# Turning q and k on VectorE instead of TensorE, with 32x32 score tiles and a re-planned instruction order

## The chip, the cores and the metric

The kernel runs on one core of a Trainium2 chip. The core has a matrix engine (TensorE, PE in the profile, with PEld for its weight loads), a vector engine (VectorE, DVE), an activation engine (ScalarE, ACT), a general engine (GpSimd, POOL) and a queue engine (SyncE, SP) that issues transfers. The metric is the time on the device in microseconds.

## The reference

Nystrom attention on q, k, v of shape [8 batches, 8 heads, 576 tokens, 64], then a mixture of experts over the 4608 tokens of width 512.

```
q_lm, k_lm = means over 18 consecutive tokens (32 landmarks)
A = softmax(q k_lm^T / 8);  Bm = softmax(q_lm k_lm^T / 8);  C = softmax(q_lm k^T / 8)
Z = iterated inverse of Bm (6 steps);  x = A Z C v, heads side by side
e = argmax(x w_gate);  out = p_e * sigmoid(x w_output_gate)_e * relu(x w1[e]) w2[e]
```

There are 8 experts with w1 [512, 1024] and w2 [1024, 512]. All tensors are float32 in memory.

## The kernel before

The work goes by batch, and inside a batch by two halves of four heads. The function batch (L367 to L762) does not issue anything: it registers operations with a planner, P.op, with an assumed duration for each engine that may do it, the buffers it takes, and a priority. Plan.run (L124 to L219) is a list scheduler that runs while the kernel is built: it takes the operation that can begin first, near ties by priority, chooses the engine that ends it earliest (shy adds a handicap to an engine), and the resulting order is written out as the fixed instruction order of each engine. Attention of batch b has priority b, its feed-forward b + 3.5.

For each half:
- k, q and v come by one transfer each on SP's queue (L378), 96 partitions, six tokens of each head in a partition (1536 B runs).
- q and k are turned on PE: 24 transposes of 96x96 (L390) into the two-bank buffers S, then copied out by ACT or DVE (L345, L351) into Tq and Tk, with two tokens' 64 channels on 128 partitions.
- Sums over 18 tokens: nine by DVE (L414, L417) or POOL (L420 to L424), then the two halves of the partitions are swapped and added (sw, L435) to give the landmarks lm.
- Scores of C (L446) and of A (L491): each 8 products of 64 rows x 32 columns with 288 moving columns; a float32 product is two matmul instructions.
- C: maximum (L452), scaling (L453), exponential (L455), six transposes on PE (L463), copy ECT, product with v (L475), scaled by the reciprocal (L480, L481).
- A: 32x32 block turn on DVE (L495), maximum (L498), subtraction on POOL (L503), exponential (L505), sum and reciprocal (L509, L510), multiplication on POOL (L512), block turn back (L516) to AT.

For each batch: scores of Bm (L527) and its normalisation (L533 to L560), seven inverse steps on PE and DVE (L573, L580 to L585), the gate product (L606), logits (L618), routing on DVE (L637 to L686), and x transposed in bf16 (L699). POOL's queue then asks for the main expert's weights, cast to bf16 (w1 in three transfers, L312 and L315; w2 in one, L720); from batch 2 on they are skipped where the expert is already there. Feed-forward: up (L734) in 16 groups of four matmuls with relu on ACT (L343), down (L749) in five row blocks of eight, scaled (L756, L758) and stored by SP (L761). Tokens of other experts go through a branch at the end (L782 on).

PSUM's eight banks are split into S (two buffers of two banks), M (two, attention) and F (two, feed-forward).

Of the kernel before, what the change touches and what calls it, by code (L numbers as in the profile page):

```python
# [37 lines left out]
class Val:  # L38


    def __init__(self, tag):
        self.tag = tag
        self.slot = None
        self.users = set()
# [9 lines left out]
class Tag:  # L54
    def __init__(self, name, tiles, ordered=True):
        self.name = name
        self.tiles = tiles
        self.held = [None] * len(tiles)
        self.free_at = [0.0] * len(tiles)
        self.ordered = ordered  # L60
        self.made = []
        self.given = 0


class Op:
    __slots__ = ("engs", "fn", "deps", "new", "vals", "prio", "lag", "end", "eng", "nd", "succ", "load", "seq",
                 "mode", "bias", "shy")


class Plan:  # L70
# [3 lines left out]
    LAT = 180.0  # L74
    PE_LAG = 50.0
    SWITCH = 95.0
    WINDOW = 3410.0
    IDLE = 0.5

# [5 lines left out]
    def op(self, engs, fn, r=(), w=(), hold=(), prio=0.0, lag=0.0, load=0.0, mode=None, after=(), bias=0.0, shy=()):  # L85
        o = Op()
        o.engs, o.fn, o.prio, o.lag, o.load = engs, fn, prio, lag, load
        o.end = None
        o.mode = mode
        o.bias = bias  # L90
# [33 lines left out]
    def run(self):  # L124
# [16 lines left out]
        filled = {}  # L141
        while ready:
            cands = []
            for o in ready:
# [3 lines left out]
                for v in o.new:  # L148
                    tg = v.tag
                    if tg.ordered and tg.made[tg.given] is not v:  # L150
                        ok = False
# [71 lines left out]
def kernel(  # L223
# [28 lines left out]
    SHY = 800.0  # L252
    SHYF = 300.0
# [28 lines left out]
    t_n = {x: tag(f"n{x}", 3, [PT, HH, 6 * D]) for x in "qkv"}  # L282
    t_T = {x: tag(f"T{x}", 2, [128, 3 * HH * PT]) for x in "qk"}
    t_s3 = tag("s3", 1, [128, HH * PT])
    t_s9 = tag("s9", 2, [128, 2, 128])
    t_lm = tag("lm", 3, [128, 2, 128])
    t_sw = tag("sw", 1, [128, 2, 128])
# [5 lines left out]
    t_X = tag("X", 3, [128, 2, m + D])  # L293
    t_sm = tag("sm", 6, [128, 64])
# [15 lines left out]
    def ask_w1(dst, e, **new):  # L310
        w = moe_w1[bass.ds(e, 1)]
        nc.gpsimd.dma_start(out=dst[:, :2], in_=w.rearrange("e (c p) f -> p (e c) f", p=128)[:, :2], **new)  # L312
        src = w.rearrange("e (c a p) f -> a p (e c) f", a=2, p=D)
        for a in range(2):
            nc.gpsimd.dma_start(out=dst[a * D:(a + 1) * D, 2:], in_=src[1 - a, :, 2:], **new)  # L315

    with tc.manual_schedule():
# [7 lines left out]
        nc.gpsimd.iota(ri, pattern=[[S, B], [128, NT]], base=0, channel_multiplier=1)  # L325
        nc.vector.tensor_copy(rows, ri)
        nc.vector.tensor_scalar(out=e8, in0=e0, scalar1=8.0, scalar2=None, op0=ADD)
        for hf in range(2):
            nc.sync.dma_start(out=wgs[hf * D:(hf + 1) * D, :, :E],
                              in_=moe_w_gate[hf * HH * D:(hf + 1) * HH * D].rearrange("(h d) e -> d h e", d=D))  # L330
            nc.sync.dma_start(out=wgs[hf * D:(hf + 1) * D, :, E:],
                              in_=moe_w_output_gate[hf * HH * D:(hf + 1) * HH * D].rearrange("(h d) e -> d h e", d=D))
        nc.vector.tensor_scalar(out=wgs[:, :, E:], in0=wgs[:, :, E:], scalar1=-1.0, scalar2=None, op0=MUL)
# [19 lines left out]

        def turned(T, x):
            if x == "k":
                return T.t.rearrange("p (j n) -> p j n", j=3)
            return T.t.rearrange("p (n j) -> p j n", j=3)

# [3 lines left out]
        def dve(n=0):  # L362
            return {"DVE": 100 + max(40, 1.05 * n)}

        xTs, coms = {}, {}

        def batch(b):  # L367
            pr = float(b)
# [3 lines left out]
            vns = []  # L372
            for hf in range(2):
                pr = b + 0.1 * hf
                ns = {}
                for x, src in (("k", k), ("q", q), ("v", v)):
                    n = ns[x] = Val(t_n[x])
                    P.op({"SP": 60}, lambda e, n=n, src=src, hf=hf: nc.sync.dma_start(  # L378
                        out=n.t, in_=src[b, hf * HH:(hf + 1) * HH].rearrange("h (p t) d -> p h (t d)", t=6)),
                        w=[n[0]], prio=pr, lag=2000, load=2300)  # L380
                vns.append(ns["v"])
                Ts = {"q": Val(t_T["q"]), "k": Val(t_T["k"])}
                order = [("k", 0), ("k", 1), ("k", 2), ("q", 0), ("q", 1), ("q", 2)]
                for a in range(3):
                    tp = Val(p_S)
                    two = order[2 * a:2 * a + 2]
                    for i, (x, j) in enumerate(two):
                        def turn(e, x=x, j=j, i=i, tp=tp, n=ns[x]):
                            for h in range(HH):
                                nc.tensor.transpose(tp.t[:, i, h * PT:(h + 1) * PT],  # L390
                                                    in_=n.t[:, h, j * 128:(j + 1) * 128], identity=I128[:PT, :PT])
                        P.op({"PE": 332}, turn, r=[ns[x][0]], w=[tp[i]], hold=[Ts[y] for y, _ in two], mode=(128, 128), prio=pr + .01)
                    if two[0][0] == two[1][0]:
                        x, j = two[0]
                        T = Ts[x]
                        P.op(evac(768), copy_to(lambda T=T, j=j, x=x: turned(T, x)[:, j:j + 2],
                                                lambda tp=tp: tp.t[:, :, :HH * PT]),
                             r=[tp[0], tp[1]], w=[T[j], T[j + 1]], prio=pr + .01)
                    else:
                        for i, (x, j) in enumerate(two):  # L400
                            T = Ts[x]
                            P.op(evac(384), copy_to(lambda T=T, j=j, x=x: turned(T, x)[:, j],
                                                    lambda tp=tp, i=i: tp.t[:, i, :HH * PT]),
                                 r=[tp[i]], w=[T[j]], prio=pr + .01)
                s9 = Val(t_s9)
                for i, x in enumerate("qk"):
                    T = Ts[x]
                    s3 = Val(t_s3)

                    def sums(e, T=T, s9=s9, s3=s3, i=i, x=x):  # L410
                        f = turned(T, x)
                        if e == "DVE":
                            if x == "k":
                                nc.vector.tensor_reduce(  # L414
                                    s9.t[:, i], f.rearrange("p j (r w) -> p r j w", w=3), axis=XY, op=ADD)
                            else:
                                nc.vector.tensor_reduce(  # L417
                                    s9.t[:, i], T.t.rearrange("p (r w) -> p r w", w=9), axis=X, op=ADD)
                            return
                        nc.gpsimd.tensor_tensor(s3.t, f[:, 0], f[:, 1], op=ADD)  # L420
                        nc.gpsimd.tensor_tensor(s3.t, s3.t, f[:, 2], op=ADD)
                        c = s3.t.rearrange("p (n w) -> p n w", w=3)
                        nc.gpsimd.tensor_tensor(s9.t[:, i], c[:, :, 0], c[:, :, 1], op=ADD)
                        nc.gpsimd.tensor_tensor(s9.t[:, i], s9.t[:, i], c[:, :, 2], op=ADD)  # L424
                    P.op({"POOL": 2900, "DVE": 1350}, sums, r=[T[0], T[1], T[2]], w=[s9[i], s3[0]], prio=pr + .02, shy={"DVE": SHY})
                lm = Val(t_lm)
                lms.append(lm)
                sw = Val(t_sw)
                for c in range(2):
                    P.op({"POOL": 480, "DVE": 260, "ACT": 390},  # L430
                         copy_to(lambda c=c, sw=sw: sw.t[c * D:(c + 1) * D], lambda c=c, s9=s9: s9.t[(1 - c) * D:(2 - c) * D]),
                         r=[s9[0], s9[1]], w=[sw[c]], prio=pr + .02, shy={"DVE": SHYF})

                def folded(e, lm=lm, s9=s9, sw=sw):
                    (nc.gpsimd if e == "POOL" else nc.vector).tensor_tensor(lm.t, s9.t, sw.t, op=ADD)  # L435
                P.op({"POOL": 730, "DVE": 370}, folded, r=[s9[0], s9[1], sw[0], sw[1]], w=[lm[0]], prio=pr + .02, shy={"DVE": SHYF})

                pC = Val(p_S)
                EC = Val(t_EC)
                st = Val(t_sm)  # L440
                sms.append(st)

                def c_scores(e, pC=pC, lm=lm, T=Ts["k"]):
                    for h in range(HH):
                        for t2 in range(2):
                            nc.tensor.matmul(pC.t[h * m:(h + 1) * m, t2, :U2],  # L446
# [398 lines left out]
```

## Time and profile before

| what | value |
|---|---|
| median of three runs | 335.58 us (334.67 to 338.91) |
| profiled execution: time, span | 333.46 us, 331.8 us |
| PE busy, 4270 matmul instructions | 287.8 us |
| PEld busy | 182.8 us |
| DVE busy | 192.0 us |
| ACT busy | 174.7 us |
| POOL busy | 85.2 us |
| moved by DMA | 48.95 MB, 147 GB/s on average |

Busy time is the union of the instructions of an engine. In a group's row the columns are: line, engine, operation, output<-input, shapes and count; then busy time and mean ns of one; then the idle time just before, with what ended it. In a timeline row they are: start, duration, engine, line, operation. Matmul ends are modelled and overlap, so distances between starts tell more.

### The profile page before, as it was taken

What the parts mean: (1) busy time and instruction counts of PE and PEld (TensorE: products, weight loads), DVE (VectorE), ACT (ScalarE), POOL (GpSimd) and SP (SyncE); (2) the same over time, 40 slices, a digit from 0 to 9 for tenths busy, and PEclk for the clock granted to TensorE, in tenths of its full rate; (3) what the DMA queues carried; (4) which work ended last, traced back from release to release, by engine and by line L of the source; (5) the groups of instructions that cost most, each with busy time, mean ns of one, the idle gap of its engine ahead of it and who ended that gap; (6) DMA issues with size and microseconds to landing.
All of it is one profiled execution on the core that took longest, in us unless ns stands there. A gap on an engine that the chain in (4) does not pass through costs nothing. (4 is left out here: it accounts for less than half of the span.)

```text
span 331.8 us, 10174 instructions
## 1 busy us (share of the span) xinstructions
PE 287.8 (87%) x4270; PEld 182.8 (55%) x4281; DVE 192.0 (58%) x526; ACT 174.7 (53%) x370; POOL 85.2 (26%) x126
## 2 busy tenths in 40 slices
PE   0576868799979989899978998999999998999994
PEld 0545655566656665657644575666565555454551
DVE  1258928977987388729866669784968626000000
ACT  1344526537845457537654566465764345454542
POOL 1034642237153024214331402330221311010000
PEclk9999779769999999999999999999999999999999
DMA  4999999289999978076730455665000946949103
GB/s 96 247 247 245 250 213 233 49 187 227 229 182 232 261 225 193 9 212 178 167 85 2 134 154 123 139 104 167 2 18 2 219 84 99 177 113 200 51 33 112
DMA packets 33584, 48.95 MB, mean 147 GB/s; under 512 B 2816, under 2 KB 26368, under 8 KB 33536
## 3 DMA queue, kind: packets, MB, share of 16 engines
q1 hardware_dynamic: 25536, 37.79, 44.4%
q0 software_dynamic: 8000, 10.49, 19.7%
q8 instruction: 34, 0.56, 0.7%
q14 instruction: 14, 0.11, 0.1%
HBM read 61.90 MB, written 9.44 MB: 215 GB/s over the span
## 5 line engine op out<-in xcount | busy, mean ns | idle before, releaser
L734 PE MATMUL F<-xT_all,w 128*128 128x288 bf16 x512 | 76.1, 286 | 2.1 <-ACT y L756 1.1
L749 PE MATMUL F<-w,hT 128*128 128x512 bf16 (+1 forms) x310 | 73.2, 380 | 1.0 <-ACT y L756 0.3
L734 PEld LDWEIGHTS <-w 128*128 128x128 bf16 x512 | 47.4, 98 | 24.1 <-issue 11.7
L343 ACT ACTIVATE hT<-F 128x288 bf16<-128x288 f32 x128 | 50.0, 411 | 16.8 <-PE F L734 14.9
L749 PEld LDWEIGHTS <-hT 128*128 128x128 bf16 (+1 forms) x320 | 30.7, 100 | 35.0 <-issue 2.8
L756 ACT ACTIVATE y<-F,co 128x512 f32<-128x512 f32 (+1 forms) x38 | 26.1, 686 | 42.4 <-PE F L749 36.6
L390 PE MATMUL S<-I,nk 96*128 96x96 f32 x192 | 25.2, 275 | 14.2 <-DMA nk<-in_k_dram 11.2
L573 PE MATMUL M<-X 32*32 32x96 f32 x768 | 26.5, 251 | 5.3 <-issue 3.2
L503 POOL TENSOR_TENSOR At<-At,sm 128x576 f32<-128x576 f32 x16 | 18.5, 1156 | 49.1 <-DVE sm L498 27.5
L390 PEld LDWEIGHTS S<-I,nk 96*128 96x128 f32 x192 | 21.1, 160 | 17.1 <-issue 9.0
L345 ACT COPY Tq<-S 128x768 f32<-128x768 f32 (+1 forms) x23 | 22.9, 1004 | 11.1 <-PE S L390 11.1
L390 PE MATMUL S<-I,nq 96*128 96x96 f32 x192 | 24.6, 270 | 2.1 <-DVE Tk L351 1.8
L345 ACT COPY Tk<-S 128x384 f32<-128x384 f32 (+1 forms) x25 | 15.6, 633 | 20.0 <-PE S L390 19.5
L512 POOL TENSOR_TENSOR At<-At,sm 128x576 f32<-128x576 f32 x16 | 18.5, 1159 | 28.2 <-DVE sm L510 10.3
L583 DVE SCALAR_TENSOR_TENSOR X<-X,M 128x192 f32<-128x192 f32 x40 | 13.7, 344 | 19.6 <-PE M L573 19.4
L573 PEld LDWEIGHTS M<-X 32*32 32x32 f32 x768 | 15.7, 105 | 16.7 <-issue 7.8
L417 DVE TENSOR_REDUCE s<-Tq 128x128 f32<-128x1152 f32 x14 | 18.9, 1350 | 8.8 <-ACT Tq L345 8.7
L390 PEld LDWEIGHTS S<-I,nq 96*128 96x128 f32 x192 | 20.4, 156 | 5.7 <-DVE Tk L351 2.4
L345 ACT CAST xT_all<-S 128x576 bf16<-128x576 f32 x28 | 16.7, 641 | 11.3 <-PE S L699 11.2
L455 ACT ACTIVATE EC<-S,sm 128x576 f32<-128x576 f32 x16 | 11.8, 740 | 18.3 <-DVE sm L453 16.7
L435 POOL TENSOR_TENSOR lm<-s,sw 128x256 f32<-128x256 f32 x12 | 8.7, 725 | 41.1 <-ACT sw L345 34.4
L345 ACT COPY ECT<-S 96x768 f32<-96x768 f32 x14 | 11.1, 796 | 14.9 <-PE S L463 14.8
(118 smaller groups left out, 395.0 us busy)
## 6 DMA issues: line engine op xcount, KB each, us to landing
nk<-in_k_dram SPq DMA_DIRECT2D x16, 576.0 KB, 8.8
nq<-in_q_dram SPq DMA_DIRECT2D x16, 576.0 KB, 8.4
nv<-in_v_dram SPq DMA_DIRECT2D x16, 576.0 KB, 8.0
w<-in_moe_w_dram POOLq DMA_DIRECT2D x8, 1024.0 KB
out_dram<-y SPq DMA_DIRECT2D x32, 256.0 KB, 2.7
w<-in_moe_w_dram POOLq DMA_DIRECT2D x8, 512.0 KB
w<-in_moe_w_dram POOLq DMA_DIRECT2D x16, 256.0 KB
out_dram<-y SPq DMA_DIRECT2D x8, 128.0 KB, 2.4
```

What stands on the lines that cost most here:

```text
L343: nc.scalar.activation(out=dst(), in_=src(), func=RELU)
L345: nc.scalar.copy(dst(), src())
L390: nc.tensor.transpose(tp.t[:, i, h * PT:(h + 1) * PT], in_=n.t[:, h, j * 128:(j + 1) * 128], identity=I128[:PT, :PT])
L417: nc.vector.tensor_reduce(s9.t[:, i], T.t.rearrange("p (r w) -> p r w", w=9), axis=X, op=ADD)
L455: P.op({"ACT": 900}, lambda e, pC=pC, EC=EC, st=st: nc.scalar.activation(out=EC.t, in_=pC.t[:, :, :U2], func=EXP, scale=s_a, bias=st.t[:, ...
L503: P.op({"POOL": 1160}, lambda e, At=At, st=st: nc.gpsimd.tensor_tensor(At.t, At.t, b_l(st.t[:, 8:8 + g]), op=SUB), r=[st["ax"]], w=[At[0]] ...
L512: P.op({"POOL": 1160}, lambda e, At=At, st=st: nc.gpsimd.tensor_tensor(At.t, At.t, b_l(st.t[:, 32:32 + g]), op=MUL), r=[st["as"]], w=[At[0 ...
L573: nc.tensor.matmul(pN.t[r_, hf * W:(hf + 1) * W], lhsT=cur.t[r_, hf, :m], rhs=cur.t[r_, hf, :])
L583: nc.vector.scalar_tensor_tensor(out=nxt.t, in0=cur.t, scalar=2.0, in1=p3, op0=MUL, op1=SUB)
L734: nc.tensor.matmul(ph.t[:, :NH], lhsT=w1.t[:, dc, fc * 128:(fc + 1) * 128], rhs=xT.t[:, dc, n * NH:(n + 1) * NH], start=(dc == 0), stop=(d ...
L749: nc.tensor.matmul(py.t[:tk, :], lhsT=hTs[fc].t[:, i * 128:i * 128 + tk], rhs=w2.t[:, fc, :], start=(fc == 0), stop=(fc == FCH - 1))
L756: nc.scalar.activation(out=y.t[:tk], in_=py.t[:tk, :], func=COPY, scale=com.t[:tk, i:i + 1])
```

## The change

- q and k come with 18 tokens of one head and landmark in a partition (128 partitions, 4608 B runs). DVE turns them in 32x32 blocks straight into Tq and Tk, whose partitions are (head, 32 channels), with the two channel halves side by side. PE no longer turns them and no engine copies them.
- The sums of 18 tokens are taken from the loaded layout by five adds on POOL or DVE, and then turned once by DVE into lm.
- Both scores become one operation of 32 float32 products of 32 rows x 32 columns, in two accumulated channel halves. It takes both S buffers. C's rows are rotated by two heads.
- v comes in three transfers, with tokens in an order that suits ECT. Tokens then stand in (18, 32) order down to the output, whose store picks rows 18 apart.
- w1 and w2 are asked for in halves; up and down wait for the half that they need.
- The gate weights are loaded after the second half's inputs, no longer first.
- M and F become one pool of four banks, attention and feed-forward capped at two each; from batch 5 on the feed-forward may take four.
- The planner has other latencies and priorities, counts PE's instruction records, and lets a fetch of 256 take no less than 3.8 us. The inverse of batch 0 is done in two halves. C's scaling moves to ACT, some small copies may go to ACT or POOL.

```diff
-    LAT = 180.0
-    PE_LAG = 50.0
+    LAT = 90.0
+    PE_LAG = 150.0
+    CHUNK = 256
+    FETCH = 3800.0
...
+                if recs // self.CHUNK != (recs + o.recs) // self.CHUNK:
+                    part = (self.CHUNK - recs % self.CHUNK) / o.recs
+                    at = max(st + part * (en - st), chunk_at + self.FETCH)
+                    en = at + (1.0 - part) * (en - st)
+                    chunk_at = at
+                recs += o.recs
...
+    PR = [0.0, 1.0, 2.0, 3.0, 4.0, 5.0, 6.0, 7.0]
+    FR = [3.5, 4.5, 5.5, 5.25, 7.5, 8.5, 9.5, 10.5]
+    PESUM = 0
+    SPLIT = (0,)
+    CAPA = 2
+    CAPF = 2
+    LASTF = 5
...
-    p_M = tag("M", 2, [128, 512], ps=True, ordered=False)
-    p_F = tag("F", 2, [128, 512], ps=True, ordered=False)
+    p_M = tag("M", 4, [128, 512], ps=True, ordered=False)
...
+                        if x == "v":
+                            for w in range(3):
+                                nc.sync.dma_start(out=n.t[w * m:(w + 1) * m],
+                                                  in_=s_.rearrange("h (r w t) d -> w r h (t d)", w=3, t=6)[w])
+                        else:
+                            nc.sync.dma_start(out=n.t, in_=s_.rearrange("h (r t) d -> (h r) t d", t=g))
...
-                            for h in range(HH):
-                                nc.tensor.transpose(tp.t[:, i, h * PT:(h + 1) * PT],
-                                                    in_=n.t[:, h, j * 128:(j + 1) * 128], identity=I128[:PT, :PT])
+                for x in "kq":
+                    P.op({"DVE": 1370}, lambda e, T=Ts[x], n=ns[x], x=x: nc.vector.transpose(
+                        out=T.t.rearrange("p j (t r) -> p t j r", r=m) if x == "q" else
+                        T.t.rearrange("p j (t w r) -> p w t j r", t=6, w=3),
+                        in_=n.t.rearrange("p t (j c) -> p t j c", j=2) if x == "q" else
+                        n.t.rearrange("p (w t) (j c) -> p w t j c", j=2, w=3)),
+                        r=[ns[x][0]], w=[Ts[x][0]], prio=pr + .01)
...
+                    def sums(e, n=ns[x], s9=s9, s3=s3, i=i):
+                        eng = nc.gpsimd if e == "POOL" else nc.vector
+                        eng.tensor_tensor(s3.t, n.t[:, :9], n.t[:, 9:], op=ADD)
+                        eng.tensor_tensor(s3.t[:, :4], s3.t[:, :4], s3.t[:, 4:8], op=ADD)
+                        eng.tensor_tensor(s3.t[:, :2], s3.t[:, :2], s3.t[:, 2:4], op=ADD)
+                        eng.tensor_tensor(s3.t[:, 0], s3.t[:, 0], s3.t[:, 1], op=ADD)
+                        eng.tensor_tensor(s9.t[:, i], s3.t[:, 0], s3.t[:, 8], op=ADD)
+                    P.op({"POOL": 3200, "DVE": 1750}, sums, r=[ns[x][0]], w=[s9[i], s3[0]], prio=pr + .005, shy={"DVE": SHY})
...
+                def scores(e, pC=pC, pA=pA, lm=lm, Ts=Ts):
+                    for n in range(2):
+                        for j in range(2):
+                            for h in range(HH):
+                                r_ = slice(h * m, (h + 1) * m)
+                                o = (h + 2) % HH
+                                nc.tensor.matmul(pC.t[o * m:(o + 1) * m, n, :U2], lhsT=lm.t[r_, 0, j, :],
+                                                 rhs=Ts["k"].t[r_, j, n * U2:(n + 1) * U2], start=(j == 0), stop=(j == 1))
+                                nc.tensor.matmul(pA.t[r_, n, :U2], lhsT=lm.t[r_, 1, j, :],
+                                                 rhs=Ts["q"].t[r_, j, n * U2:(n + 1) * U2], start=(j == 0), stop=(j == 1))
...
-            P.op({"POOL": 1200}, ask1, r=[em[0]], w=[w1[0]], prio=pr + .06, lag=2000, load=8100)
+            for part in range(2):
+                P.op({"POOL": 1500}, lambda e, part=part: ask1(e, part), r=[em[0]], w=[w1[part]], hold=[w2], prio=pr + .06,
+                     lag=2000, load=WLOAD / 2)
...
-                    out=out[b * S + i * 128:b * S + i * 128 + tk, :], in_=y.t[:tk]), r=[y[0]], prio=fr, lag=2000, load=900)
+                    out=out[b * S:(b + 1) * S].rearrange("(r t) d -> t r d", t=g)[HH * i:HH * i + tk // m], in_=y.t[:tk]), r=[y[0]], prio=fr, lag=2000, load=900)
```

More of the change, by code (lines that the diff above doesn't have):

```diff
@@ L89, in op @@
         o.mode = mode
+        o.recs = recs
         o.bias = bias
@@ L150, in run @@
                     if tg.ordered and tg.made[tg.given] is not v:
+                        ok = False
+                        break
+                    if sum(x is not None and x.kind == v.kind for x in tg.held) >= v.cap:
                         ok = False
@@ L352, in copy_to, with bring_gates @@
             return emit
[L354 to L357, printed above, removed]
         def evac(n):
             return {"ACT": 140 + 0.95 * n, "DVE": 90 + 1.1 * n}
-        def dve(n=0):
-            return {"DVE": 100 + max(40, 1.05 * n)}
         xTs, coms = {}, {}
+        gates = Val(None)
+        def bring_gates(e):
+            for hf in range(2):
+                for i, w in enumerate((moe_w_gate, moe_w_output_gate)):
+                    nc.sync.dma_start(out=wgs[hf * D:(hf + 1) * D, :, i * E:(i + 1) * E],
+                                      in_=w[hf * HH * D:(hf + 1) * HH * D].rearrange("(h d) e -> d h e", d=D))
         def batch(b):
-            pr = float(b)
+            pr = PR[b]
             lms, ATs, sms, ZVp = [], [], [], []
@@ new lines, in batch @@
+                    P.op({"SP": 550 if x != "v" else 1500}, bring, w=[n[0]], prio=pr if x != "v" else pr + .15, lag=2000, load=LOAD)
+                if b == 0 and hf == 1:
+                    P.op({"SP": 2500}, bring_gates, w=[gates[0]], prio=pr, lag=2500)
+                    P.op({"POOL": 400}, lambda e: nc.gpsimd.tensor_scalar(
+                        out=wgs[:, :, E:], in0=wgs[:, :, E:], scalar1=-1.0, scalar2=None, op0=MUL),
+                        w=[gates[0]], prio=pr + .5)
+                Ts = {"q": Val(t_T["q"]), "k": Val(t_T["k"])}
@@ L426, in batch @@
                 lm = Val(t_lm)
                 lms.append(lm)
[L428 to L435, printed above, removed]
@@ L436, in batch @@
[L436 to L438 removed]
+                P.op({"DVE": 270}, lambda e, lm=lm, s9=s9: nc.vector.transpose(
+                    out=lm.t.rearrange("p x j r -> p (x j r)"),
+                    in_=s9.t[:, :128] if b < PESUM else s9.t.rearrange("p x d -> p (x d)")),
+                    r=[s9[0], s9[1]], w=[lm[0]], prio=pr + .02)
+                pC, pA = Val(p_S), Val(p_S)
@@ L439, in batch @@
                 EC = Val(t_EC)
+                At = Val(t_At)
                 st = Val(t_sm)
                 sms.append(st)
[L443 to L446, printed above, removed]
-                                             lhsT=lm.t[t2 * D:(t2 + 1) * D, 0, h * m:(h + 1) * m],
-                                             rhs=turned(T, "k")[t2 * D:(t2 + 1) * D, :, h * PT:(h + 1) * PT])
@@ new lines, in c_rec @@
+                def c_rec(e, st=st):
+                    for a in range(2):
+                        nc.vector.reciprocal(st.t[a * D:(a + 1) * D, 3:4], st.t[(1 - a) * D:(2 - a) * D, 2:3])
+                P.op({"DVE": 280}, c_rec, r=[st[1]], w=[st[2]], prio=pr + .035)
+                def pv_out(e, pV=pV, st=st, hf=hf):
+                    if e == "ACT":
+                        nc.scalar.activation(out=XW.t[:, hf, m:], in_=pV.t[:, :D], func=COPY, scale=st.t[:, 3:4])
+                    else:
+                        nc.vector.tensor_scalar(out=XW.t[:, hf, m:], in0=pV.t[:, :D], scalar1=st.t[:, 3:4],
+                                                scalar2=None, op0=MUL)
@@ L725, in batch @@
+            for part in range(2):
+                P.op({"POOL": 1500}, lambda e, part=part: ask1(e, part), r=[em[0]], w=[w1[part]], hold=[w2], prio=pr + .06,
+                     lag=2000, load=WLOAD / 2)
+            for part in range(2):
+                P.op({"POOL": 500}, lambda e, part=part: ask_w2(w2.t, reg["e"], part, **reg["new"]),
+                     r=[w1[0], w1[1]], w=[w2[part]], prio=pr + .06, lag=2000, load=WLOAD / 2)
+            fr = FR[b]
             hTs = []
@@ L780 @@
     gi = pool.tile([128, NT], I32, name="gi")
-    xg = pool.tile([128, DCH, S], BF16, name="xg")
+    xg = t_hT.tiles[FCH:FCH + DCH]
     with tc.If(strays > 0):
         with tc.For_i(0, B) as bi:
-            nc.vector.tensor_copy(xg, xT_all[:, bass.ds(bi, 1)].rearrange("p a c s -> p (a c) s"))
+            for dc in range(DCH):
+                nc.vector.tensor_copy(xg[dc], xT_all[:, bass.ds(bi, 1), dc].rearrange("p a s -> p (a s)"))
             for i, src in enumerate((eid_all, co_all, rows)):
@@ L790 @@
                 with tc.If(flag > 0):
-                    ask_w1(w1, ei_)
-                    nc.gpsimd.dma_start(out=w2, in_=moe_w2[bass.ds(ei_, 1)].rearrange("e (c p) d -> p (e c) d", p=128))
+                    for part in range(2):
+                        ask_w1(w1, ei_, part)
+                        ask_w2(w2, ei_, part)
                     nc.vector.tensor_copy(gen[:, 3, :1], e0[:, bass.ds(ei_, 1)])
```

293 lines of the change are left out of this document (130 added, 163 removed).

## Prediction, on record before the run

> **What bounds the kernel now.** I read the page's slices first, then its costliest groups, then the timeline of single engines.
>
> ```profile
> PE   0576868799979989899978998999999998999994
> DVE  1258928977987388729866669784968626000000
> PEclk9999779769999999999999999999999999999999
> DMA  4999999289999978076730455665000946949103
> ```
>
> A slice is 8.3 us. TensorE (PE) is nearly full from slice 10 to the end; the first 80 us are the weak part. VectorE (DVE) is done at 281 us, 46 us before the last matmul: what is left then is a backlog of feed-forward work on PE. So PE's work is the bound after the first 80 us, and a chain of short steps before. The table by stretches says: PE busy 55.26 of the first 80 us, 187.08 of the next 200, 45.47 of the last 52.
>
> ```profile
> L734 PE MATMUL F<-xT_all,w 128*128 128x288 bf16 x512 | 76.1, 286 | 2.1 <-ACT y L756 1.1
> L390 PE MATMUL S<-I,nk 96*128 96x96 f32 x192 | 25.2, 275 | 14.2 <-DMA nk<-in_k_dram 11.2
> L390 PE MATMUL S<-I,nq 96*128 96x96 f32 x192 | 24.6, 270 | 2.1 <-DVE Tk L351 1.8
> L417 DVE TENSOR_REDUCE s<-Tq 128x128 f32<-128x1152 f32 x14 | 18.9, 1350 | 8.8 <-ACT Tq L345 8.7
> ```
>
> The turning of q and k (L390) is a sixth of PE's busy time, and its first matmul waits 9.1 us for k. Ends of matmuls overlap, so I price PE by distances between starts, at full clock, from the timeline:
>
> ```profile
> 229.01 1.16 PE L390 MATMUL S<-I,nq 96*128 96x96 f32 x12
> 230.01 0.66 PE L734 MATMUL F<-xT_all,w 128*128 128x288 bf16 x4
> ...
> 237.45 0.53 PE L573 MATMUL M<-X 32*32 32x96 f32 x16
> 237.91 0.71 PE L446 MATMUL S<-Tk,lm 64*32 64x288 f32 x16
> 238.42 0.69 PE L491 MATMUL S<-Tq,lm 64*32 64x288 f32 x16
> 239.04 0.53 PE L573 MATMUL M<-X 32*32 32x96 f32 x16
> ...
> 272.36 0.74 PE L699 MATMUL S<-AT,X 32*64 32x288 f32 x16
> 273.03 1.15 PE L734 MATMUL F<-xT_all,w 128*128 128x288 bf16 x8
> ```
>
> Twelve turns take 1.00 us (four alone 0.33 to 0.43), the k scores 0.51, the q scores 0.62, one inverse step 0.46, half of the x product 0.67.
>
> **PE, per half batch (16 of them).** Removed: 24 turns, about 2.1 us, and both scores, about 1.15. Added: scores as 64 matmul instructions of 288 columns, 32 rows each, on 8 tiles of the array, against 16 and 16 on 8 tiles before: each tile now streams 8 instead of 2 and 2. From L446 (16 instructions on 8 tiles, 0.51) four times gives 2.04; from L699, which also uses 32-row tiles, 4 x 0.67 = 2.68. I take 2.2: L446 matches the output width of 32 columns, and L573 (32x32 tiles) shows little over its stream. Net -2.1 - 1.15 + 2.2 = -1.05, so -17 us in all (bounds -19 and -9). The small B scores double from 16 to 32 instructions: 8 x 0.15 = +1. PE falls by about 16 us.
>
> On the scores a rule stands against the change. L573 writes one bank from four row tiles at once, in different partitions; its 16 instructions of 96 columns stand 0.46 us apart, where one after the other, at L446's 0.51 / 2 = 0.255 us for 288 columns, they would need 16 x 0.085 = 1.36. So in this trace such tiles do run together. The Trainium skill, TensorEngine Tiling (Array Packing), section Gotcha 1: PSUM Pressure, says that different row tiles can't access one bank at the same time; the new scores write each bank from four row tiles, so by it they would run one by one in two banks, 64 x 0.255 / 2 = 8.2 us, not 2.2. L573 disagrees; it is a rival below.
>
> **DVE.** Removed: block sums 18.9 + 14.7 (L417, L414), copies of Tq, Tk on DVE 4.7 + 2.4 + 3.8 + 1.7, swap copies 3.1, fold 1.7, the scaling L453 2.5: 53.5 us. Added: 32 block turns of 1152 columns. The turn L516 takes 0.770 for 576 columns and L621 0.335 for 160, 1.05 ns a column, so 1.37 each, 43.9 us; the turned strides are new, so the price lies between 0.77 (half the columns) and twice 1.37. The landmark turn, 128 columns, 0.30 x 16 = 4.8. A second reciprocal, 2.2; split inverse of batch 0, about 1. Sums that the plan gives to DVE: by L435 (256 columns 0.43) and L638 (40 columns 0.20) five adds cost 0.76 + 0.43 + 0.29 + 0.23 + 0.23 = 1.9 each; I guess 8 of 32, 15 us (none to all: 0 to 61). DVE becomes 192.0 - 53.5 + 67 = 206 us, 25.7 a batch.
>
> **ACT and POOL.** ACT loses the copies of Tq, Tk and sw, 46 us of 174.7, and gets small operations at about 0.27 (L641) some 32 times, 9 us. POOL loses 32 us (fold, swap, its seven old sums) and gets about 24 sums: 1.16 + 0.73 + 0.49 + 0.4 + 0.35 = 3.1 by L503, L435, L424 and below, 74 us; twice as many weight transfers add up to 15 us of issue. POOL goes from 85 to about 142. Both have room, so their own cost is nothing beside PE; what would cost is a landmark that comes late from POOL, or the port: L663 takes 0.231 as a rule and 1.100 once, L638 0.200 and 0.770, each while a POOL add ran. Such stretches add up to 6.3 us now; with 1.7 times POOL's time, 10 to 11, +4 on DVE.
>
> The Trainium skill, SBUF, section Who interferes with whom, says that DVE instructions with two SBUF inputs lose whole instructions of time to GpSimd ones that read SBUF. The stretched rows agree, and by it DVE's new adds could each lose up to one POOL add, 1.16 us: 40 adds, at most 46 us more on DVE, against the 4 taken.
>
> **Front of the work.** Now k is issued at 3.69, behind four gate loads, and lands at 9.10. It becomes SP's first transfer, at 0.9, so 6.3; q 2.4 us later (576 KB at 245 GB/s), 8.7. Sum of k on POOL 6.3 to 9.4; turn of q on DVE 8.7 to 10.1; sum of q to 12.3; landmarks 12.6; scores 12.8 to 17 at the half clock that the first turns show (12 in 2.15). Before, they ended at 24.1, and the second half's at 31.6. The next half's k and q stand ahead of v now and land at 11.1 and 13.5; DVE's turns and POOL's sums set its scores at 18 to 22: 9.5 us earlier. The chain from there to the first feed-forward (31.6 to 79.5 now: softmax, inverse 39.3 to 53.9, routing, weights asked at 67.2) stays. Weights in halves let the up product start on half of w1, 1 MB less at 227 GB/s, 4.5 us (0 if SP's other loads fill the gap, 6 if both gain). First feed-forward: 79.5 - 9.5 - 4.5 = 65 us. v in three transfers costs SP 2 x 0.31 to 0.6 us more each, hidden by loads that run two halves ahead; gates are needed at 56 us now and load after the second half, hidden. The output goes in the same 2 KB rows to other places: 0 as long as y's four buffers cover 2.4 to 2.7 us; else 0.3 a row block.
>
> **Instruction fetch.** q8 shows 34 packets, 0.56 MB: 256 PE instructions each. The 3.15 us wait of L573 at 41.1 for "issue" is PE waiting with its data ready. PE's records go from 8551 to 9063 (-768 turns, +1024 scores, +256 B scores): two fetches more. I take 0: a stall less, two fetches more, between -3 and +6.
>
> **The sum**, on the profiled execution (span 331.8, time 333.46; the median shown is 335.58). After 79.5 PE had 5.5 batches of attention at 15.9 us (2 x (2.1 + 1.15 + 0.68 + 0.8) + 6.4) and 8 feed-forwards of 17.7 (64 x 0.135 + 40 x 0.227): 229. It took 248, factor 1.08. After the change 65 us in, with 2.07 batches done (59 us at 25.7 each, DVE nine tenths busy), there remain 5.93 x 13.9 + 142 = 224.5, by 1.08 242.5; the end after the last matmul is 4.5: 312. From batch 5 on the feed-forward may use four banks: alone, four up matmuls stand 0.576 apart (48 in 6.89), mixed 0.49; 16 such in two to three batches give 3 back. Span 309, time 311.
>
> **Rivals.**
> (1) DVE becomes the bound, and the kernel slower. Attention needs 206 us of it; after its last operation there remain weights (12.3 less 4.5), 17.7 of feed-forward and 2, about 27. If it is busy a share s, the end is 6 + 206 / s + 27. It decides at 0.69 (332); at 0.65 it is 350. Its share from 6 to 281 us now is 191 / 275 = 0.69, and my forecast needs 0.75. For it: this share, both new scores that need both S banks at once, and POOL's locks. Against: DVE reaches 0.94 and 0.95 in 30 to 40 and 80 to 90 us, and between 80 and 280 us, at 0.71, it was PE, 94% busy, that held the attention back, with 46 us of feed-forward left over at the end.
> (2) Freed PE time stays idle: the front is no earlier, scores cost 2.68, two fetches stall: 333 - 9 + 1 + 4 = 329, about no change. For it: PE waits in the first 80 us on ACT, DVE and DMA by turns. Against: the full slices behind.
> (3) It goes better: the inverse of batch 0 in halves and a plan with fetches save 8 us more of the chain, and half of the 13 us idle between 80 and 280: about 297.
> (4) Row tiles exclude each other in a bank: 16 x (8.2 - 2.2) = 96 more, over 400. L573 speaks against it.
>
> **How the numbers follow.** Forecast 0.62 (300 to 322 by the bounds of scores, DVE sums and front); (1) 0.16, of which 0.06 comes out level; (2) 0.07, of which 0.02 is faster; (3) 0.13; (4) 0.02. Faster by over 2% (below 328.9; 2% is about what a measurement can tell): 0.62 + 0.13 + 0.02 = 0.77; same 0.06 + 0.05 = 0.11; slower 0.10 + 0.02 = 0.12. The range 296 to 328 takes in (3) and the forecast's bounds.
>
> **What would show it.** Right: no L390 turns; a score group of 1024 matmuls about 2.2 us apart per half; DVE turns of 1.37; first feed-forward near 65 us; PE busy near 270; DVE near 206. Wrong: DVE turns near 2.7 us, scores near 2.7 or 8, PE waiting for DVE between 80 and 250 us, or DVE still busy 30 us before the end.

## The result, and the profile after

The changed kernel takes 339.47 us (median of 20 runs, 335.08 to 343.01) beside 335.1 us for the kernel before (20 runs, 331.49 to 340.39): ratio 1.012, 95% interval 1.008 to 1.017. The forecast was 311 us, range 296 to 328. Ratios and their intervals, here and below, are of the fast runs of each kernel alone, while medians are of all its runs, so the two differ a little. The profiled execution shown here took 341.74 us, with a span of 340.1 us and a mean granted TensorE clock of 0.913 (0.973 before).

First the slices of the changed kernel's page, 8.5 us each; they answer to the first lines shown of before.

```profile
PE   0466755896998799599899997399999975996950
DVE  4698978797897896689816936459441430500000
PEclk9956969699999799899999999789999995999795
DMA  7999747559958977476212315817021159196221
```

TensorE (PE) has holes near 140, 215 and 280 us, where it was nearly full before, and its last slice is empty. From 136 us on, each slice with a granted clock under 9 is one of these holes, comes right behind one, or is the last; in the first experiment below, a clock of 0.948, still lower than before, goes with 314 us, which speaks against the clock as a cause of its own. Now the costliest groups of the same page.

```profile
L759 PE MATMUL M<-xT_all,w 128*128 128x288 bf16 x512 | 75.2, 298 | 19.3 <-DMA w<-in_moe_w_dram 11.9
...
L459 PE MATMUL S<-Tk,lm 32*32 32x288 f32 x512 | 43.6, 467 | 11.4 <-DVE lm L442 11.4
...
L415 DVE STREAM_TRANSPOSE Tk<-nk 128x1152 f32<-128x1152 f32 x16 | 21.7, 1358 | 0.1
L415 DVE STREAM_TRANSPOSE Tq<-nq 128x1152 f32<-128x1152 f32 x16 | 21.5, 1346 | 0.0
```

The parts that the change was priced by are as priced: a turn on DVE takes 1.35 us, and PE is busy for 265.4 us (287.8 before), DVE for 199.5 (192.0), ACT for 146.3 (174.7), POOL for 137.7 (85.2). What is new is in the first row: the up products (L759) stand idle for 19.3 us, most of it for weights; before (L734) it was 2.1 us, half of it for y. The waits of PE in the changed kernel (total, times, longest) put it in order:

```profile
PE M L759 <- DMA w<-in_moe_w_dram: 11.9, 4, 4.4
...
PE M L759 <- DVE X L602: 4.3, 2, 3.4
PE M L759 <- ACT y L781: 2.9, 1, 2.9
```

Why would ACT be late with y? The timeline of ACT at the end of the changed kernel says it:

```profile
313.27 0.68 ACT L781 ACTIVATE y<-M,co 64x512 f32<-64x512 f32 x1 [5.12 <-DMA out_dram<-y]
...
325.77 0.69 ACT L781 ACTIVATE y<-M,co 128x512 f32<-128x512 f32 x1 [0.18 <-PE M L774]
328.74 0.68 ACT L781 ACTIVATE y<-M,co 64x512 f32<-64x512 f32 x1 [2.29 <-PEq L807]
```

At 313 us ACT waits 5.12 us for a store (out_dram<-y) to free one of y's four buffers, and after the last scaling, which ends at 329.4, the span goes on for 10.7 us. Before, the same row is this, and 3.9 us remain to 331.8:

```profile
327.27 0.68 ACT L756 ACTIVATE y<-F,co 64x512 f32<-64x512 f32 x1 [1.16 <-PEq L782]
```

So the theory after the look at the traces was S: the store is slow. Its rivals were W (weights are asked for too late by the new plan) and D (DVE is the new bound, rival 1 of the prediction).

### The profile page after: what moved, and what is told of

Same layout as the page of the kernel before. It is cut to its first block, busy times and chain, and to the rows that moved or that the text cites. A ratio compares the mean times of both kernels' runs of the same rounds, so it can differ in the third digit from the quotient of the medians.

```text
span 340.1 us, 10916 instructions
## 1 busy us (share of the span) xinstructions
PE 265.4 (78%) x4525; PEld 169.9 (50%) x4537; DVE 199.5 (59%) x542; ACT 146.3 (43%) x356; POOL 137.7 (40%) x225
## 5 line engine op out<-in xcount | busy, mean ns | idle before, releaser
L759 PE MATMUL M<-xT_all,w 128*128 128x288 bf16 x512 | 75.2, 298 | 19.3 <-DMA w<-in_moe_w_dram 11.9
L774 PE MATMUL M<-w,hT 128*128 128x512 bf16 (+1 forms) x309 | 73.6, 381 | 0.6
L759 PEld LDWEIGHTS <-w 128*128 128x128 bf16 x512 | 50.3, 102 | 38.5 <-issue 12.6
L365 ACT ACTIVATE hT<-M 128x288 bf16<-128x288 f32 x128 | 50.4, 410 | 31.6 <-PE M L759 27.4
L459 PE MATMUL S<-Tk,lm 32*32 32x288 f32 x512 | 43.6, 467 | 11.4 <-DVE lm L442 11.4
L461 PE MATMUL S<-Tq,lm 32*32 32x288 f32 x512 | 41.1, 465 | 0.0
L781 ACT ACTIVATE y<-M,co 128x512 f32<-128x512 f32 (+1 forms) x38 | 25.8, 685 | 34.1 <-PE M L774 24.7
L459 PEld LDWEIGHTS S<-Tk,lm 32*32 32x32 f32 x512 | 25.2, 119 | 18.3 <-DVE lm L442 11.1
L434 POOL TENSOR_TENSOR s<-nk 128x576 f32<-128x576 f32 x13 | 18.3, 1407 | 14.9 <-DMA nk<-in_k_dram 8.0
L415 DVE STREAM_TRANSPOSE Tk<-nk 128x1152 f32<-128x1152 f32 x16 | 21.7, 1358 | 0.1
L415 DVE STREAM_TRANSPOSE Tq<-nq 128x1152 f32<-128x1152 f32 x16 | 21.5, 1346 | 0.0
## 6 DMA issues: line engine op xcount, KB each, us to landing
nv<-in_v_dram SPq DMA_DIRECT2D x48, 192.0 KB
```

The lines of the kernel that those rows point to most:

```text
L365: nc.scalar.activation(out=dst(), in_=src(), func=RELU)
L415: P.op({"DVE": 1370}, lambda e, T=Ts[x], n=ns[x], x=x: nc.vector.transpose(out=T.t.rearrange("p j (t r) -> p t j r", r=m) if x == "q" else ...
L434: eng.tensor_tensor(s3.t, n.t[:, :9], n.t[:, 9:], op=ADD)
L459: nc.tensor.matmul(pC.t[o * m:(o + 1) * m, n, :U2], lhsT=lm.t[r_, 0, j, :], rhs=Ts["k"].t[r_, j, n * U2:(n + 1) * U2], start=(j == 0), sto ...
L461: nc.tensor.matmul(pA.t[r_, n, :U2], lhsT=lm.t[r_, 1, j, :], rhs=Ts["q"].t[r_, j, n * U2:(n + 1) * U2], start=(j == 0), stop=(j == 1))
L759: nc.tensor.matmul(ph.t[:, :NH], lhsT=w1.t[:, dc, fc * 128:(fc + 1) * 128], rhs=xT.t[:, dc, n * NH:(n + 1) * NH], start=(dc == 0), stop=(d ...
```

## The experiments

**The store alone, back to contiguous rows.** The same order of instructions; the output's rows land in the order in which the tokens are worked on, so the return to their own places is left out.

```diff
-  out=out[b * S:(b + 1) * S].rearrange("(r t) d -> t r d", t=g)[HH * i:HH * i + tk // m], in_=y.t[:tk])
+  out=out[b * S + i * 128:b * S + i * 128 + tk, :], in_=y.t[:tk])
```

> The changed kernel in the same instruction order, with only the output's store put back to 128 rows in one piece. It leaves out the put-back of token order, so rows stand at other places of the output. Theory S (the store of rows 18 apart is spread over few transfer engines): descriptors go back from about 52 to over 100 per us, the end comes about 4 instead of 11 us after the last scaling, and the wait of the up product for y (2.9 us at 314) goes: 7 to 11 us faster than the changed kernel (ratio to the kernel before 0.98 to 0.99). Theory W (the plan expects weights too early) and theory D (VectorE is the bound): only the tail moves, at most 3 us, 1.00 to 1.01.

Measured 314.51 us (ratio 0.942, 0.937 to 0.948). One line of code is worth 25 us (23 by the two ratios), more than twice the 7 to 11 that theory S expected. The page of this kernel has this row for the up products:

```profile
L759 PE MATMUL M<-xT_all,w 128*128 128x288 bf16 x512 | 74.2, 296 | 4.3 <-DMA w<-in_moe_w_dram 2.8
```

and its tail is back at 3.9 us (the last scaling ends at 308.4, the span at 312.3).

**The store as four stores of 32 rows, all rows in their own places.**

```diff
-  nc.sync.dma_start(out=...rearrange("(r t) d -> t r d", t=g)[HH * i:HH * i + tk // m], in_=y.t[:tk])
+  [nc.sync.dma_start(out=...rearrange("(r t) d -> t r d", t=g)[HH * i + j], in_=y.t[j * m:(j + 1) * m])
+   for j in range(tk // m)]
```

> The changed kernel with each output store issued as four stores of 32 rows (two for the last), each with the rows outermost; the result stays the reference's. Theory S: each small store is spread over all transfer engines, so the same 7 to 11 us are won, less up to 2 us for four issues of 0.54 us on SyncE at the end (0.98 to 0.995). If rows 18 apart were slow in themselves, nothing is won (1.01). Theory W and D: at most 3 us.

Measured 319.59 us (0.948, 0.940 to 0.957), again far more than the 7 to 11 us expected. Rows that lie 18 apart are thus not what makes the store slow; the form of the one instruction is.

**Weights planned later, and both edits together.**

```diff
-    WLOAD = 5000.0
+    WLOAD = 8100.0
...
-                     lag=2000, load=WLOAD / 2)
+                     lag=4500, load=WLOAD / 2)
```

> The changed kernel with only the planner's figures for weight transfers changed (a half lands 8.55 us after its issue instead of 4.5), so that the first up product is placed about 10 us after the request, as the trace of the changed kernel shows it landing. Theory W: PE's waits for weights (11.9 us in total, with half-clock matmuls behind them) fall below 4 us, the last batch's chain is no longer held up behind them, and 6 to 14 us are won (0.97 to 0.995). Theory S: the tail of 11 us stays and the gain is under 4 us (1.00 or more). Theory D: nothing, since VectorE's work stays (1.01).

> Both of the last two edits. Theories S and W together: the gains add, 13 to 24 us from the changed kernel (0.94 to 0.975). If VectorE is the bound, about 1.00, with VectorE over 0.75 busy up to its last operation.

Measured 341.71 us (1.024, 1.017 to 1.031) for the later weights alone: PE no longer waits for them, but 5.7 us for y in three places, and the tail is 11 us. With the store in parts too, 325.58 us (0.973, 0.967 to 0.980), 6 to 8 us more than with the parts alone (by medians and by ratios): the gains do not add. W falls: the plan's due times are not the cause. D falls too, since the run with contiguous rows has the same work on DVE.

**The same store in the kernel before.**

```diff
-  out=out[b * S + i * 128:b * S + i * 128 + tk, :], in_=y.t[:tk])
+  out=out[b * S:(b + 1) * S].rearrange("(r t) d -> t r d", t=g)[HH * i:HH * i + tk // m], in_=y.t[:tk])
```

> The kernel before with one edit: its stores have the shape of the changed kernel's (4 tokens of 32 rows that lie 18 apart, 2 tokens in the last one); nothing else is changed. It leaves out that each row lands in its own place: rows of the output change places, the amount written is the same. Theory S (the shape alone makes a store slow, about 2.4 us at 53 descriptors a microsecond instead of 1 at 133, in any kernel): the tail after the last scaling goes from 3.9 to about 10.5 us, weights come late as in the changed kernel, 345 to 358 us, ratio 1.03 to 1.07. Rival V (it cost 25 us only because the new plan asks for weights in halves and later against its need): the tail alone, 6 to 7 us, ratio 1.02. Rival O (the order of the planner's instructions is what matters, not the shape): no change, 1.00.

Measured 342.6 us (1.021, 1.005 to 1.037): 7 us, theory V. In the profile its tail is 10.5 us instead of 3.9, and PE waits for weights and y no longer than before (the up products are idle for 2.0 us). So the store's price depends on what lies beside it: the w2 packets of the last two experts take 11.1 and 13.0 us here instead of 7.7 and 7.3, but where 51 us of feed-forward are left after the last routing (280.9 to 331.8 before), late weights are covered, and only the tail is paid.

**Stores alone, by shape.** The whole computation is left out.

```
for a in (1, 2, 4, 8, 16, 32):        # last: four stores of 32 rows, as dst[j] of a = 4
    for many in (1, 8):
        nc.vector.memset(y, 1.0)
        for i in range(many):
            dst = out[i * 128:(i + 1) * 128]        # a > 1: .rearrange("(r t) d -> t r d", t=a)
            nc.sync.dma_start(out=dst, in_=y)
```

> Stores alone: the whole computation is left out. For each shape, one store of 128 rows of 2 KB from 128 partitions, then eight in a row, with a wait between. The rows go to a block of 128 in DRAM as 1 x 128, 2 x 64, 4 x 32, 8 x 16, 16 x 8 and 32 x 4 (outermost dimension first), and last as four stores of 32 rows each, whose rows lie 4 apart as in 4 x 32. Theory S (a store is dealt to as many of the 16 transfer engines as its outermost dimension counts): eight stores take about 8 us as 1 x 128, 16 x 8 and 32 x 4, 10 as 8 x 16, 20 as 4 x 32 (1024 descriptors at 52 a microsecond), 40 as 2 x 64; the four parts take about 8 to 10 again, though their rows lie apart. Rival A (rows that lie apart in DRAM are slow): all of them but 1 x 128 take 20, the four parts too.

The timeline of DVE in this kernel; the bracket is the wait until the stores before it have landed. Rows go in pairs: after one store, after eight.

```profile
3.74 0.48 DVE L56 MEMSET y<- 128x512 f32 x1 [2.35 <-DMA out_dram<-y]
11.30 0.48 DVE L56 MEMSET y<- 128x512 f32 x1 [7.07 <-DMA out_dram<-y]
19.90 0.48 DVE L56 MEMSET y<- 128x512 f32 x1 [8.12 <-DMA out_dram<-y]
64.52 0.48 DVE L56 MEMSET y<- 128x512 f32 x1 [44.13 <-DMA out_dram<-y]
71.14 0.48 DVE L56 MEMSET y<- 128x512 f32 x1 [6.14 <-DMA out_dram<-y]
96.28 0.48 DVE L56 MEMSET y<- 128x512 f32 x1 [24.66 <-DMA out_dram<-y]
101.03 0.48 DVE L56 MEMSET y<- 128x512 f32 x1 [4.26 <-DMA out_dram<-y]
115.93 0.48 DVE L56 MEMSET y<- 128x512 f32 x1 [14.42 <-DMA out_dram<-y]
119.54 0.48 DVE L56 MEMSET y<- 128x512 f32 x1 [3.12 <-DMA out_dram<-y]
129.15 0.48 DVE L56 MEMSET y<- 128x512 f32 x1 [9.13 <-DMA out_dram<-y]
132.31 0.48 DVE L56 MEMSET y<- 128x512 f32 x1 [2.67 <-DMA out_dram<-y]
140.47 0.48 DVE L64 MEMSET y<- 128x512 f32 x1 [7.68 <-DMA out_dram<-y]
144.34 0.48 DVE L64 MEMSET y<- 128x512 f32 x1 [3.38 <-DMA out_dram<-y]
```

Eight stores of the same 2 MB take 7.1 us as 1 x 128, 44.1 as 2 x 64, 24.7 as 4 x 32, 14.4 as 8 x 16 (10 expected), 9.1 as 16 x 8 and 7.7 as 32 x 4. The time falls by a factor of 1.6 to 1.8 with each doubling of the outermost dimension from 2 to 16, and all but the first lay rows apart in DRAM: theory S, not A. Eight times four parts end 17.5 us after their memset (144.8 to the end of the program at 162.3), more than the 8 to 10 expected; the 32 issues stand in one queue, and in the kernel row blocks come further apart.

How many transfer engines a store uses can, it seems, be read in the kernels' pages too. SP's queue carries, beside the data, packets of 4 bytes, and their number changes with the shape alone. These are the rows of queue q1 in the changed kernel, with contiguous rows, and in parts:

```profile
q1 hardware_dynamic: 17360, 37.79, 35.9%
```

```profile
q1 hardware_dynamic: 17856, 37.79, 40.0%
```

```profile
q1 hardware_dynamic: 19520, 37.80, 41.0%
```

The first two differ by 496 = 32 x (16 - 4) + 8 x (16 - 2): 40 stores with 16 such packets each against 4, and 2 for the half blocks. The third has 144 stores of 16, and 144 x 16 - 40 x 16 = 1664 = 19520 - 17856. The kernel before with the store by token has 25040, 496 less than before's 25536. The Trainium skill, DMA: Bandwidth & Descriptors, section Why a DMA increments its semaphore by 16 and not by 1, states the rule: a transfer uses the largest number of engines up to 16 that divides the slowest dimension of both sides. The runs agree in all seven forms: the trace of the stores alone has 16, 2, 4, 8, 16 and 16 such packets for each store, in the order of the loop, and 16 for each part.

**Where the 25 us arise.** By token in batch 7 alone, contiguous in the others (whose rows then don't land in their own places).

```diff
+  dst = (out[b * S + i * 128:b * S + i * 128 + tk, :] if b < B - 1 else
+         out[b * S:(b + 1) * S].rearrange("(r t) d -> t r d", t=g)[HH * i:HH * i + tk // m])
```

> The changed kernel with its stores to contiguous rows in batches 0 to 6 and by tokens, as in the changed kernel, in batch 7 alone. It leaves out that the rows of the first seven batches land in their own places. It splits the 25 us that all stores cost (339.5 against 314.5). Theory S2 (the tail and the y buffers cost 6 to 7 us, the rest is earlier batches' stores on four transfer engines that make weights and loads late): 320 to 323 us. Rival T (all of it is the last batch): 335 us or more.

Measured 322.47 us (0.966, 0.955 to 0.976): theory S2. The last batch's stores cost 8 us (314.5 to 322.5), the earlier ones 17 (322.5 to 339.5). In this kernel's profile, PE waits for weights little more than with contiguous rows (2.8 us), and the end is slow as in the changed kernel:

```profile
PE M L759 <- DMA w<-in_moe_w_dram: 4.1, 3, 2.8
```

```profile
309.00 0.68 ACT L781 ACTIVATE y<-M,co 64x512 f32<-64x512 f32 x1 [1.97 <-DMA out_dram<-y]
```

From 309.7 to the end at 320.8 it is 11.1 us. Where the other 17 us arise can be read from the two traces, since the order of instructions is the same: the changed kernel's PE is within 3 us of this one's up to 137 us, and its lag then grows in four places, to 4.5 us by 145, 11 by 222, 15 by 282 and 19 by 318 us (the profiled execution is 2 us slower than the median). These are the waits behind it; the first is POOL's, which holds up a turn on DVE for 5.2 us and so PE, at 140 us, for 3.4. With batch 7 alone by token, that sum starts at 127.7 us, without a wait.

```profile
133.16 1.40 POOL L434 TENSOR_TENSOR s<-nk 128x576 f32<-128x576 f32 x1 [5.65 <-DMA nk<-in_k_dram]
...
217.51 0.66 PE L759 MATMUL M<-xT_all,w 128*128 128x288 bf16 x2 [4.42 <-DMA w<-in_moe_w_dram]
...
281.88 0.66 PE L759 MATMUL M<-xT_all,w 128*128 128x288 bf16 x2 [3.73 <-DMA w<-in_moe_w_dram]
...
314.00 4.69 PE L759 MATMUL M<-xT_all,w 128*128 128x288 bf16 x24 [2.89 <-ACT y L781]
```

So one part is a load of k that lands late, two are weights, and the last is y. The data packets of the changed kernel show these transfers side by side with stores. Where they are alone, the stores of full row blocks land about 50 packets in each us (327 to 333 us). From 113 to 123 us they land about 24; beside them 164 to 175 weight packets land in each us up to 117, and from 118 to 123 only about 24, so that the last part of the weights goes at the stores' pace. That the weights' and loads' packets on the stores' few engines take turns with the stores is the likeliest reading; the records don't name the engine of a packet, so it isn't shown.

**Rest of the prediction, on top of the store in parts.** The halves of the weights, with the plan made for whole ones, and with the plan's order kept:

```diff
-  for part in range(2):
-      P.op({"POOL": 1500}, lambda e, part=part: ask1(e, part), r=[em[0]], w=[w1[part]], ...)
+  P.op({"POOL": 1500}, lambda e: [ask1(e, part) for part in range(2)], r=[em[0]], w=[w1[0], w1[1]], ...)
...
# in the second run, in ask_w1: the whole w1 is asked for at the place of its first half
+  if part:
+      return
```

> The changed kernel with the store in four parts, and each expert's weights asked for as whole w1, then whole w2 in the plan (one operation for both halves; up products wait for both). The prediction priced the halves at 4.5 us of the first feed-forward. By it: first up product 3 to 5 us later, near 78 us, and about 323 us, ratio to the run with the store in parts 1.01. Rival (other loads fill the gap, halves are worth nothing): 319 to 320 us.

> The changed kernel with the store in four parts and the plan's order on every engine kept, but each expert's w1 comes as one whole at the place of its first half, and w2 too: the up and down products wait for all of it. It is the halves alone, without the new order that the planner makes of whole weights, which took 335.9 us. By the prediction the halves are worth 4.5 us at the first feed-forward and less later: 323 to 326 us against 319.6. Rival (the halves are worth nothing, and the 16 us of the run with whole weights in the plan are the planner's order): 318 to 321 us.

Measured 335.88 us (1.000, 0.994 to 1.006) with the plan for whole weights, 326.46 with its order kept (beside 337.93 for before on that chip; without an interval). The halves alone are worth 4 to 7 us (by shares of before on the same chip, and by medians), about as expected, but not where the prediction put them: with whole asks the first up product stands at the same place (the row of the up products up to 110 us, whole asks first, then the run with batch 7 by token), and PE's waits for weights over the whole run are 10.4 us instead of 4.0.

```profile
L760 PE MATMUL M<-xT_all,w x80: 282/286/297, 73.7 to 109.0; 128*128 128x288 bf16 x80
```

```profile
L759 PE MATMUL M<-xT_all,w x72: 283/286/297, 73.8 to 102.5; 128*128 128x288 bf16 x72
```

That the other 9 us of the plan for whole weights are the planner's order is only what is left over; no run shows it.

The sums of q and k in the first three batches, once by 18 matmuls on PE, once cut to one add (16 of the 18 tokens of those landmarks are left out):

```diff
-    PESUM = 0
+    PESUM = 3
```

```diff
+    if b < 3:
+        eng.tensor_tensor(s9.t[:, i], n.t[:, 0], n.t[:, 9], op=ADD)
+        return
```

> The changed kernel with the store in four parts, and the sums of q and k of the first three batches made by TensorE (18 matmuls by the identity that add up in one bank, instead of five adds on POOL or VectorE). Theory F (the first feed-forward comes at 74 us and not at 65 because VectorE and POOL, which share the sums, are full from 16 to 50 us): landmarks of the second half come some 4 us earlier, first feed-forward at 67 to 70 us, 312 to 317 us against 319.6 with the store in parts alone. Rival P (the chain of batch 0 is not waiting for sums, and TensorE has no room for 12 x 2.05 us): first feed-forward at 73 us or later, 320 to 330 us.

> The changed kernel with the store in four parts, in the same order of instructions, but with one add of 64 columns in place of the five adds of each sum in the first three batches. It leaves out 16 of the 18 tokens of those landmarks. Theory F (the first feed-forward stands at 74 us and not at 65 because VectorE and POOL are full of sums in the first 50 us): VectorE saves about 1.7 us for each of its sums and POOL 2.9, the second half's landmarks come 4 us earlier, first feed-forward at 66 to 70 us, 311 to 316 us against 319.6. Rival P (the chain of batch 0 is delayed by the turns and scores of batches 1 and 2 that the plan puts between its steps, not by the sums): first feed-forward at 72 us or later, 317 to 320 us.

On PE the sums say nothing about DVE: 363.87 us, as the two halves' sums of k alone keep PE from 5.1 to 20.7 us; all twelve sums come to 64.8 us of PE, not 25 (12 x 2.05). Cut short: 316.47 us (before on that chip: 337.93). The second half's scores start at 19.0 us (23.8 with batch 7 alone by token, 24.5 in parts), and the first up product at 70.6 (73.8 and 75.6), so F holds for 3 to 5 us of the front.

```profile
L762 PE MATMUL M<-xT_all,w x80: 282/286/297, 70.6 to 108.6; 128*128 128x288 bf16 x80
```

**Parts on two queues.**

```diff
-  [nc.sync.dma_start(...) for j in range(tk // m)]
+  [(nc.sync, nc.scalar)[j % 2].dma_start(...) for j in range(tk // m)]
```

> The changed kernel with the store in four parts, two of them issued by SyncE and two by ScalarE; order of the rest kept. Theory S (what is left against the run with contiguous rows, 319.6 to 314.5 us, is four issues in a row on one queue): the tail after the last scaling goes from about 7 to 5 us, 316 to 318 us. Rival (ScalarE's issues come at the cost of its copies): 320 to 324 us.

Measured 324.25 us (318.8 to 324.97, before on that chip 337.93): no gain. The tail goes from 7.0 to 4.3 us, but PE now waits 3.5 us for relu (hT) on ACT. The store in four parts on SP remains the fastest of the kernels measured that leave nothing out.

## Why the prediction was wrong

**The step that failed** is a sentence at the end of the front's paragraph: "The output goes in the same 2 KB rows to other places: 0 as long as y's four buffers cover 2.4 to 2.7 us". It took the landing time of the old store for the new one, since size and rows were the same. By the packets and the rule above, the new store is dealt to 4 transfer engines (2 in the half blocks), not 16: alone it takes 6.1 us instead of 2.4 in the experiment, and eight in a row 24.7 instead of 7.1. It lands late, holds y's buffers, and a load of k and weights come late beside it. The term was put at 0, at most 0.3 us a row block; it is 25 us (339.5 against 314.5). With contiguous rows the kernel takes 314.5 us, within 4 of the 311 forecast, and with the rows in their own places, in parts, 319.6: the store alone took the time out of the range. The cover named, y's buffers, was also too narrow: loads and weights do not go through them. The rule stood in the Trainium skill's section cited above; the prediction read the store by its bytes and not by its outermost dimension. That the rest came within 4 us is in part luck, since two other misses nearly cancel (see the front, below).

**PE held.** It was to fall by 16 us to near 270; it fell by 22 to 265.4. The timeline of the changed kernel has the disputed scores at full clock:

```profile
209.59 0.42 PE L461 MATMUL S<-Tq,lm 32*32 32x288 f32 x4
209.70 0.51 PE L459 MATMUL S<-Tk,lm 32*32 32x288 f32 x4
209.83 0.42 PE L461 MATMUL S<-Tq,lm 32*32 32x288 f32 x4
209.94 0.51 PE L459 MATMUL S<-Tk,lm 32*32 32x288 f32 x4
```

Eight tiles start anew every 0.24 us, and all 64 instructions take 2.0 us (208.81 to 210.80), not 8.2: rival 4 fell. The rule of the Trainium skill, TensorEngine Tiling (Array Packing), section Gotcha 1: PSUM Pressure, does not hold here, for row tiles that write different partitions of a bank.

**DVE, ACT and POOL held.** Turns 1.35 us for 1.37, 10 sums on DVE for the 8 guessed, 199.5 us busy for 206; POOL 137.7 for 142; ACT 146.3 for 138 (174.7 less 46 and 9 more). Of the ten first adds on DVE, eight take 0.72 to 0.76 us; one takes 2.15 and one 1.56, each beside a POOL operation on At. That is 2.2 us in all, and the smaller adds take 0.43, 0.29 and twice 0.23 on average, as priced: far from the 46 us at most. Rival 1 did not decide: with the same DVE work the contiguous store gives 314.5 us. The fetch term, put at 0, does not show either: PE waits 0.4 us for issue in all, 2.7 with contiguous rows, 3.6 before. The late landmark that the prediction feared from POOL is there in a small way: in that kernel a sum on DVE waits for POOL, and the second half's scores start only at 23.9 us.

```profile
16.14 0.76 DVE L434 TENSOR_TENSOR s<-nq 128x576 f32<-128x576 f32 x1 [3.62 <-POOL s L438]
```

**The front was too hopeful by 9 us.** The first scores came at 11.4 us (12.8 forecast) and, at half clock, took 3.8 (4.2 forecast). With contiguous rows, the second half's came at 23.9 to 27.8 instead of 18 to 22, and from their end to the first up product it is 46.1 us (27.8 to 73.9), the 47.9 of before almost unchanged. Of the 9 us, the late second half is some 6, and the 4.5 us of the halves did not come there. Five of the nine are made good behind: from the first up product to the end of the last scaling it is 234.5 us (73.9 to 308.4), 248.5 before (79.5 to 328.0), 239.5 forecast (65 to 304.5, there to the last matmul).

**The outcome** fell among the cases within 2%, which got 0.11; but rival 2, which was to end there, is not what happened: freed PE time was used, and then lost again to a transfer.

## What to carry to other kernels

When a change touches the access pattern of a transfer, look first at the slowest dimension on both sides: with 2, 4 or 8 there, the stores of this case went to that many engines by the small packets of their queue, and took longer accordingly. Price a slow store not only by the buffer it holds, but by the transfers in flight beside it, and ask what backlog covers those. The gain of a re-tiling can be real and be hidden by one line at its far end; undo that line alone, with the order of instructions kept, before the plan is blamed.

## What was not expected of the hardware

The same 2 MB take 7.1 or 44.1 us by the shape of the store alone, and the last part of a weight transfer beside such stores lands 24 packets in a us, after 164 to 175. A sum of 18 rows by matmuls with the identity takes PE 5.4 us in float32 (64.8 us for twelve), though each matmul moves 64 columns only; the planner's price was 2.05.
